# The first two steps of a scan-and-feed-forward kernel on half of the tokens, with the other half's scan between them

## The chip, the cores and the metric

The kernel runs on one core of one Trainium2 chip. Its time is the device time of one execution in microseconds (us). Before the change three executions took 386.27, 387.29 and 387.14 us; the median is 387.14 us. The execution that the profiler recorded has a span of 384.9 us, and all times inside it count from the start of that span.

## The reference

Two blocks follow each other. The first is a Mamba-2 style scan (SSD) over x of 4 sequences, 8 heads, 768 positions, head width 32, with a state of width 16; the second is a feed-forward block with a gate, over the 3072 rows that come out.

```
for each chunk:                       # the reference uses chunks of 32, the kernel of 128
    cum = cumsum(log(clip(a)))
    M   = (C @ B.T) * exp(cum_i - cum_j) * (i >= j)
    y   = M @ x  +  (C @ state) * exp(cum_i)
    state = exp(sum) * state + sum_j B_j x_j exp(cum_last - cum_j)

x2 = y as 3072 rows of 256            # 4 sequences x 768 positions, 8 heads x 32
h  = x2 @ w_in                        # 256 -> 2048
g  = h * cos(h)
out = g @ w_out                       # 2048 -> 256
```

The weights w_in and w_out arrive as 64-bit floats, everything else as 32-bit ones.

## The kernel before, in words

**Tiling.** A chunk is 128 positions of all four sequences, so 512 tokens; there are NC = 6 chunks. Inside a chunk the feed-forward block runs in NF = 16 steps. A step n takes one half u of the tokens (two sequences, 256 tokens) and one pair j of the 16 column blocks of w_in (256 of the 2048 hidden columns). `first(n)` makes h for them: four matmuls of 128x256, two (over the halves of the 256 inputs) for each block e of the pair. Then ScalarE makes k, the whole turns in h (`L516`), VectorE the rest of the turn, w (`L518`), ScalarE the cosine (`gate`, `L523`) and VectorE the product gT (`gated`, `L528`). `second(n)` multiplies gT with w_out into an accumulator in PSUM; it stands two steps behind its `first` (LAG = 2).

**The order is written by hand.** The kernel is built under a manual schedule: each engine runs its instructions in the order in which the Python code calls them. [...]

**The start.** Chunk 0 has no state behind it, and its scan is done sequence by sequence (b = 0 to 3) ahead of the first step. For one sequence: `spread_a` (TensorE puts a's decays in place), `decays0` (one VectorE scan, `L308`, then two GpSimd instructions, `L311` and `L312`), `turn` (TensorE turns B and C, ScalarE makes cT twice and bT of them), `cross` (one matmul for two sequences, and two ScalarE copies into lam, `L320`), `intra` (four matmuls g, then two VectorE products m, `L380`), and `finish` (eight matmuls y, and a ScalarE copy into yT, `L394`, which is the operand of `first`). `weigh` (GpSimd, `L327`) prepares `sum_up`, the matmuls that make the chunk's state; `carry` stores that state for the next chunk. `fill` is a matmul without use that keeps TensorE busy.

**The weights.** Each weight comes in eight pieces of 512 KB (`fetch`). A piece is turned into 32-bit floats by `grade` (ScalarE `L193` and `L191`, GpSimd `L194`) and `join` (VectorE `L207` and `L209`, GpSimd `L217`). The first piece of w_in is graded in two shares. Piece i of w_in holds the columns of the pair j = i; piece i of w_out the rows of the pair j = i.

**Before the change** all four scans stand ahead of `first(0)`, except `finish(3)` and the states, which stand right behind it. In chunk 0 the steps take the halves in turn: `turn_of` gives n = 0 the pair 0 of the first half, n = 1 the pair 0 of the second half, n = 2 the pair 1 of the first half, and so on. So the second piece of w_in is first used at n = 2, and the second half of the tokens at n = 1. All loads go through one queue in the order of the code: B, C and x of the sequences 0, 1 and 2, the first piece of w_in, B, C and x of sequence 3, a_in, and then pieces of both weights in turn. `a_in` is all of a; from it GpSimd makes `cut` and `la`, which go back to memory as a_cut and a_all and are read again as the decays of the chunks from 1 on.

**Buffers.** PSUM is held by tags with two buffers each: "h" for the results of `first` (and at the start for spread_a and turn), "o" for those of `second` (and at the start for cross and finish), and "scan", two buffers of two banks, for g, tp and the states.

Of the kernel before, what the change touches and what calls it, by code (L numbers as in the profile page):

```python
# [25 lines left out]
def kernel(  # L26
# [29 lines left out]
    nc = tc.nc  # L56
    V, ACT, G, PE = nc.vector, nc.scalar, nc.gpsimd, nc.tensor

    NB, H, S, D = x.shape
# [48 lines left out]
    def load(c, seqs=(0, NB)):  # L108

        if c >= NC:  # L110
            return
        if c not in raw:
            raw[c] = (loads.tile([P, 2, NB * H, N], FP32, tag="bc", name="bc"),
                      loads.tile([P, NB, H, D], FP32, tag="xr", name="xr"))
        bc, xr = raw[c]
        xr = xr.rearrange("p b h d -> p (b h) d")
        rs = slice(seqs[0] * H, seqs[1] * H)
        for dst, src in ((bc[:, 0, rs], B), (bc[:, 1, rs], C), (xr[:, rs], x)):
            nc.sync.dma_start(out=dst, in_=src[seqs[0]:seqs[1], :, c * P:(c + 1) * P, :]
                              .rearrange("b h s n -> s (b h) n"))  # L120
# [96 lines left out]
            G.tensor_tensor(out=dst.bitcast(U32), in0=bits, in1=last, op=ALU.add)  # L217

    for b in range(NB):
        if b == NB - 1:  # L220
            fetch("in", 0)
        load(0, (b, b + 1))
    nc.sync.dma_start(
        out=a_in, in_=a.rearrange("(u b) h (c p) -> (b h c) u p", u=NU, p=P))
    for w in (("in", 1), ("out", 0), ("in", 2), ("out", 1), ("in", 3)):
        fetch(*w)


# [73 lines left out]
    def decays0(b):  # L302
# [8 lines left out]
        G.tensor_copy(out=l[W:P, 1], in_=l[W:P, 0])  # L311
        G.memset(l[W:P, 0], 0.0)  # L312

    def cross(b, tag):

        ps = bank([P, H, W], "l_ps", tag)
        PE.matmul(ps, lhsT=fros[:, b:b + 2].rearrange("p b j -> p (b j)"), rhs=tos,
                  start=True, stop=True)
        for t in range(2):
            ACT.copy(out=lam[0, b + t][0:W, 1], in_=ps[t * W:(t + 1) * W])  # L320
            weigh(0, b + t)

    def weigh(c, b):

        scaled[c, b] = sc = scan.tile([P, H, N], FP32, tag="sc", bufs=NB, name="sc")
        l = lam[c, b][:, :, P - 1:P] if c > 0 else lam[c, b][:, 1, :, W - 1:W]
        G.tensor_tensor(out=sc, in0=raw[c][0][:, 0, heads(b)],  # L327
                        in1=l.to_broadcast([P, H, N]), op=ALU.mult)
# [21 lines left out]
            return  # L350
        weigh(c, b)

    def turn(b, tag=None):

        bc = raw[0][0]
        tp = (pair("tp")[:, 0] if tag is None else bank([P, 4 * P], "tp", tag)
              ).rearrange("p (k i) -> p k i", k=4)
        for k in range(2):
            PE.transpose(tp[:, k], bc[:, k, heads(b)].rearrange("p h n -> p (h n)"), ident)

        cT = scan.tile([P, 2, P], FP32, tag="cT", name="cT")
        for t in range(2):
            ACT.activation(cT[:, t], tp[:, 1], AF.Copy, scale=slot[:, t:t + 1])
        bT = scan.tile([P, P], FP32, tag="bT", name="bT")
        ACT.copy(out=bT, in_=tp[:, 0])
        part[0, b] = (bT, cT)

    def intra(b):
        bT, cT = part[0, b]
        g = [pair("g") for _ in range(2)]  # L370
        for q in range(4):
            r = slice(32 * q, 32 * q + 32)
            PE.matmul(g[q // 2][:, q % 2, 0:2 * P], lhsT=bT[r],
                      rhs=cT[r].rearrange("p t (s i) -> p s t i", s=2), start=True, stop=True)
        l = lam.pop((0, b))
        m = scan.tile([P, 2, H, W], FP32, tag="m", name="m")
        for q in range(2):
            of = [t[:, :, q * HH:(q + 1) * HH].rearrange("p s (k t) i -> p k s (t i)", k=2)
                  for t in (m, l)]
            V.tensor_tensor(out=of[0], in0=g[q][:, :, 0:2 * P].rearrange(  # L380
                "p k (s i) -> p k s i", s=2), in1=of[1], op=ALU.mult)
        part[0, b] = m

    def finish(b, tag, fills=0):
        m, xr = part.pop((0, b)), raw[0][1]
# [111 lines left out]
    def turn_of(n):  # L497

        c, f = divmod(n, NF)
        return (f % 2, f // 2) if c == 0 else divmod(f, NJ)  # L500

    def first(n):
# [6 lines left out]
        for e in range(2):  # L509
            fs = slice((2 * j + e) * P, (2 * j + e + 1) * P)  # L510
            for k in range(KT):
                PE.matmul(to_[:, e], lhsT=w_in[:, k, fs], rhs=y[:, k, u],  # L512
                          start=(k == 0), stop=(k == KT - 1), skip_group_check=True)
# [142 lines left out]

    warm = bank([P, 4, P], "warm", "o")
    fill(warm, 2)
    fill(warm[:, 0:2])
    spread_a(0, "h")  # L660
    turn(0)
    spread_a(1, "h")
    spread_a(2, "o")
    spread_a(3, "h")
    for b in range(NB):
        decays0(b)
    turn(1, "h")
    cross(0, "o")
    intra(0)
    turn(2, "h")  # L670
    cross(2, "o")
    intra(1)
    finish(0, "o")
    grade("in", 0, n=2)
    intra(2)
    turn(3, "h")
    finish(1, "o", 1)

    la = const.tile([RB, NU, P], FP32, name="la")
    cut = const.tile([RB, NU, P], FP32, name="cut")  # L680
# [7 lines left out]
    join("in", 0)  # L688
    finish(2, "o")
    intra(3)  # L690
    grade("in", 1)
    join("in", 1)


    piece = {n: ("in", (n + 3) // 2) if n % 2 else ("out", n // 2) for n in range(NF)}
# [12 lines left out]

    def first_scan():

        finish(3, "o")
# [21 lines left out]
    def halves_at(n):  # L733
        return [(c, b, t) for c in range(1, NC) for u in range(2)
                for m, b, t in ahead.get(c, {}).get(u, halves_of[u]) if m + (c - 1) * NF == n]

    EARLY = 3
    rest_of_loads()
    for n in range(NC * NF + LAG):
        c, f = divmod(n, NF)  # L740
        early = n < EARLY
        if n < NC * NF:
            if f == 0 and c > 0:
                load(c + 2)
            first(n)
            if n == 0:
                first_scan()
            for at in pairs(n):
                turn2(*at)
            rests = [grade(*piece[m], later=True)  # L750
                     for m in ((n,) if early else ()) + ((n + 1,) if n >= EARLY - 1 else ())
                     if m in piece]
            gate(n)
            for rest in rests:
                if rest:
                    rest()
            if not early and n in piece:
                join(*piece[n])
            gated(n)
            if early and n in piece:  # L760
                join(*piece[n])
            if n in (1, 2):
                carry(0, n - 1, sums[n - 1])
        for i, js in differ_at.get(n, ()):
            differ_w(i, js)
        if n >= LAG:
            second(n - LAG)
        for c, u in pairs(n - 1):
            intra2(c, u)
            masked(c, 2 * u)  # L770
        for c, u in pairs(n - 2):
            masked(c, 2 * u + 1)
        for c, u in pairs(n - 3):
# [41 lines left out]
```

## Time and profile before

| what | value |
|---|---|
| time, median of 3 | 387.14 us (386.27 to 387.29) |
| span of the profiled execution | 384.9 us |
| TensorE busy (matmul) | 378.3 us, 98% |
| VectorE busy | 265.9 us, 69% |
| GpSimd busy | 245.4 us, 64% |
| ScalarE busy | 172.9 us, 45% |
| first matmul of `first(0)` | at 18.80 us |
| first matmul of `second(0)` | at 26.55 us |

The busy time of TensorE is a share of the whole span. The change touches only the first 30 us or so, and there the question is what TensorE does in each stretch, and what it waits for. So the rows to read are those of the start, in order of time, and the list of what TensorE waited for after the start.

### The profile page before, as it was taken

The page shows a single profiled execution, that of the slowest core. Times are in us where ns is not written, and L with a number is a line of the kernel's source. Part 1 is how long each engine was busy: PE and PEld are TensorE (multiplying, and loading weights), DVE is VectorE, ACT ScalarE, POOL GpSimd, SP SyncE. Part 2 cuts the span into 40 slices and gives each one's busy share as a digit, 9 for nine tenths or more (in the row PEclk, how much of TensorE's full clock was granted, in tenths as well). Part 3 has the DMA queues.
Part 4 walks back from the last instruction along what each step waited for, and adds up shares of the span by engine and source line. Part 5 has one row for each costly group of instructions (what it writes and reads, how often), then busy time and mean ns, then how long its engine had stood idle before and what let it go on. Part 6 is the DMA issues. An engine that isn't in the chain of part 4 may idle for free.

```text
span 384.9 us, 7726 instructions
## 1 busy us (share of the span) xinstructions
PE 378.3 (98%) x2982; PEld 331.2 (86%) x2982; DVE 265.9 (69%) x395; ACT 172.9 (45%) x303; POOL 245.4 (64%) x366
## 2 busy tenths in 40 slices
PE   8999999999999999999999999999999999999996
PEld 3578887888899899899899899899899989989995
DVE  7879999678667658657657757756765865863443
ACT  3878566534334334335334434434433433433441
POOL 5757665458859549648648837855955855853751
PEclk9999999999999999999999999999999999999999
DMA  7989899975002951301791301201210000010001
GB/s 83 270 235 266 249 230 137 181 96 151 2 0 63 148 52 57 96 2 54 127 81 55 97 2 56 81 17 43 68 43 1 21 10 0 2 27 3 7 22 27
DMA packets 106371, 30.42 MB, mean 79 GB/s; under 512 B 75520, under 2 KB 102240, under 8 KB 106336
## 3 DMA queue, kind: packets, MB, share of 16 engines
q1 hardware_dynamic: 106176, 29.81, 38.9%
q8 instruction: 23, 0.38, 0.5%
q10 hardware_dynamic: 160, 0.13, 0.1%
q14 instruction: 12, 0.10, 0.1%
HBM read 26.59 MB, written 3.34 MB: 78 GB/s over the span
## 4 chain that ended last, share of the span: by engine, by line
PE 82%; DVE 7%; POOL 3%; ACT 2%; issue 2%; DMA 2%; SPq 1%; ACTq 0%
PE hp L512 37%; PE o L609 32%; PE g L422 3%; PE y L454 3%; DVE mag L209 2%; DVE w L518 2%; DMA xr<-in_x_dram 2%; PE y L447 2%; DVE lam L344 2%; PE o L571 1%; DVE gT L528 1%; PE warm L101 1%; ACT w L523 1%; PE a_ps L298 1%; PE tp L405 1%
## 5 line engine op out<-in xcount | busy, mean ns | idle before, releaser
L512 PE MATMUL hp<-yT,w_in 128*128 128x256 f32 x768 | 184.4, 383 | 0.6 <-POOL w_in L217 0.3
L512 PEld LDWEIGHTS hp<-yT,w_in 128*128 128x128 f32 x768 | 139.2, 190 | 22.7 <-issue 4.5
L553 POOL TENSOR_TENSOR gd<-gT 128x256 f32<-128x256 f32 x79 | 71.9, 911 | 89.5 <-DVE gT L528 86.2
L528 DVE TENSOR_TENSOR gT<-hp,w 128x512 f32<-128x512 f32 x96 | 66.3, 691 | 69.9 <-ACT w L523 60.1
L523 ACT ACTIVATE w<-w,quarter 128x512 f32<-128x512 f32 x96 | 69.3, 722 | 97.2 <-DVE w L518 97.2
L516 ACT ACTIVATE k<-hp 128x512 int32<-128x512 f32 x96 | 57.1, 595 | 90.8 <-PE hp L512 90.7
L518 DVE SCALAR_TENSOR_TENSOR w<-hp,k 128x512 f32<-128x512 f32 x96 | 65.4, 681 | 36.7 <-ACT k L516 36.4
L609 PE MATMUL o<-words,gd 128*128 128x128 f32 x474 | 67.0, 277 | 0.6 <-POOL gd L555 0.6
L609 PEld LDWEIGHTS o<-words,gd 128*128 128x128 f32 x474 | 59.3, 192 | 2.4 <-POOL gd L555 2.2
L344 DVE TENSOR_TENSOR_SCAN lam<-arow,unit 128x512 f32<-128x512 f32 x40 | 55.7, 1394 | 0.0
L609 PEld LDWEIGHTS o<-w_out,gT 128*128 128x128 f32 x316 | 46.9, 191 | 3.6
L609 PE MATMUL o<-w_out,gT 128*128 128x128 f32 x316 | 48.0, 274 | 0.0
L555 POOL TENSOR_TENSOR gd<-gT,gd 128x128 f32<-128x128 f32 x79 | 43.1, 546 | 6.2
L556 POOL TENSOR_TENSOR gd<-gT,gd 128x128 f32<-128x128 f32 x79 | 35.9, 455 | 6.2
L571 PE MATMUL o<-w_out,gT 128*128 128x256 f32 x128 | 30.3, 380 | 0.4 <-POOL w_out L217 0.4
L609 PE MATMUL o<-w_out,gd 128*128 128x128 f32 x158 | 30.6, 275 | 0.0
L609 PE MATMUL o<-words,gT 128*128 128x128 f32 x158 | 30.5, 275 | 0.0
L571 PEld LDWEIGHTS o<-w_out,gT 128*128 128x128 f32 x128 | 24.2, 190 | 4.0 <-POOL w_out L217 0.8
L435 DVE TENSOR_TENSOR m<-g,lam 128x512 f32<-128x512 f32 x40 | 25.6, 681 | 0.0
L624 POOL TENSOR_TENSOR sum<-ps,sum 128x256 f32<-128x256 f32 (+1 forms) x27 | 24.2, 909 | 1.4
L609 PEld LDWEIGHTS o<-w_out,gd 128*128 128x128 f32 x158 | 24.0, 192 | 0.0
L609 PEld LDWEIGHTS o<-words,gT 128*128 128x128 f32 x158 | 24.0, 192 | 0.0
(91 smaller groups left out, 293.9 us busy)
## 6 DMA issues: line engine op xcount, KB each, us to landing
arow<-a_cut SPq DMA_DIRECT2D x20, 512.0 KB
words<-in_moe_w_in_dram SPq DMA_DIRECT2D x8, 512.0 KB
words<-in_moe_w_out_dram SPq DMA_DIRECT2D x8, 512.0 KB
out_dram<-sum SPq DMA_DIRECT2D x18, 128.0 KB
xr<-in_x_dram SPq DMA_DIRECT2D x4, 512.0 KB
along<-a_all SPq DMA_DIRECT2D x20, 64.0 KB
xr<-in_x_dram SPq DMA_DIRECT2D x8, 128.0 KB
bc<-in_B_dram SPq DMA_DIRECT2D x4, 256.0 KB
```

The costliest lines, as they stand in the source:

```text
L344: V.tensor_tensor_scan(out=lam[c, b][:, hs].rearrange("p h i -> p (h i)"), data0=rows_.rearrange("p h i -> p (h i)"), data1=unit.rearrange ...
L435: V.tensor_tensor(out=of[0], in0=g[q][:, :, s * 2 * P:(s + 1) * 2 * P], in1=of[1], op=ALU.mult)
L512: PE.matmul(to_[:, e], lhsT=w_in[:, k, fs], rhs=y[:, k, u], start=(k == 0), stop=(k == KT - 1), skip_group_check=True)
L516: ACT.activation(k, hp[n], AF.Copy, bias=0.25, scale=INV_2PI)
L518: V.scalar_tensor_tensor(out=w, in0=hp[n], scalar=INV_2PI, in1=k, op0=ALU.mult, op1=ALU.subtract)
L523: ACT.activation(cos, cos, AF.Sin, bias=quarter, scale=TWO_PI)
L528: V.tensor_tensor(out=gT[n], in0=hp.pop(n), in1=cos, op=ALU.mult)
L553: G.tensor_tensor(out=d[:, 0:2], in0=g[:, 1:2].to_broadcast([P, 2, P]), in1=g[:, 3::-3], op=ALU.subtract)
L555: G.tensor_tensor(out=d[:, 2], in0=g[:, 0], in1=d[:, 0], op=ALU.subtract)
L556: G.tensor_tensor(out=d[:, 3], in0=g[:, 2], in1=d[:, 2], op=ALU.subtract)
L571: PE.matmul(o[c, u][:, t], lhsT=g[:, 2 * e + t], rhs=w_out[:, 2 * j + e], start=(j == e == t == 0), stop=(j == NJ - 1 and e == 1), skip_gr ...
L609: PE.matmul(at[q], lhsT=a_[q], rhs=w[q], start=(j == 0 and q in starts), stop=(j == NJ - 1), skip_group_check=True)
```

## The change

The kernel goes on to compute the same. Four things are moved.

- **The steps.** `turn_of` gives the first four steps of chunk 0 as (half 0, pair 0), (half 0, pair 1), (half 1, pair 0), (half 1, pair 1). So the first two steps need the sequences 0 and 1 alone, and they need two pieces of w_in.
- **The scan.** Only sequences 0 and 1 are scanned ahead of `first(0)`. `decays0` of sequences 2 and 3 stays ahead of it, and the rest of their scan is put between the parts of the first two steps by a new function `start`: `turn(2)` and `cross(2)` between the two halves of `first(0)`, `intra(2)` behind it, `turn(3)` between the two halves of `first(1)`, then `intra(3)`, `finish(2)`, `finish(3)` and the states. `turn(3)` writes into the unused half of a bank that holds g of sequence 2. `cross` is split: the matmul stays in it, the two copies go to `crossed`; the four `weigh` stand behind `gated(0)`.
- **The loads.** Two pieces of w_in are fetched behind sequence 1, ahead of sequences 2 and 3; a_in goes behind sequence 2, and then come two pieces of w_out and two of w_in.
- **The weights at the start.** Both first pieces of w_in are graded and joined ahead of `first(0)`. The first piece of w_out is graded behind `gated(0)` and joined at the end of `start`; the other pieces of the first steps are graded one step later than before. The fills change: one ahead of the scan goes, and `finish(0)` and `finish(1)` get one and two (before: none and one). `carry` of chunk 0 goes from n = 1 and 2 to n = 4 and 5.

The purpose is to let `first(0)` begin before the second pair of sequences has been loaded and scanned.

```
     for b in range(NB):
-        if b == NB - 1:
+        load(0, (b, b + 1))
+        if b == 1:
             fetch("in", 0)
-        load(0, (b, b + 1))
-    nc.sync.dma_start(
-        out=a_in, in_=a.rearrange("(u b) h (c p) -> (b h c) u p", u=NU, p=P))
-    for w in (("in", 1), ("out", 0), ("in", 2), ("out", 1), ("in", 3)):
+            fetch("in", 1)
+        if b == 2:
+            nc.sync.dma_start(
+                out=a_in, in_=a.rearrange("(u b) h (c p) -> (b h c) u p", u=NU, p=P))
+    for w in (("out", 0), ("out", 1), ("in", 2), ("in", 3)):
         fetch(*w)
...
-        return (f % 2, f // 2) if c == 0 else divmod(f, NJ)
+        if c > 0:
+            return divmod(f, NJ)
+        return divmod(f, 2) if f < 4 else (f % 2, f // 2)
...
     warm = bank([P, 4, P], "warm", "o")
     fill(warm, 2)
-    fill(warm[:, 0:2])
     spread_a(0, "h")
-    turn(0)
     spread_a(1, "h")
+    turn(0, pair("tp")[:, 0, 0:2 * P])
+    decays0(0)
+    decays0(1)
+    cross(0, "o")
+    crossed(0)
+    crossed(1)
     spread_a(2, "o")
+    intra(0)
+    turn(1, bank([P, 2 * P], "tp", "h"))
+    decays0(2)
     spread_a(3, "h")
...
+    finish(0, "o", 1)
+    grade("in", 0, n=2)
     intra(1)
...
+    grade("in", 1)
+    finish(1, "o", 2)
+    join("in", 0)
+    join("in", 1)
+    decays0(3)
...
+    def start():
+
+
+        def then():
+            turn(2, pair("tp")[:, 0, 0:2 * P])
+            cross(2, "o")
+            crossed(2)
+        first(0, then)
+        crossed(3)
+        g = intra(2)
+        first(1, lambda: turn(3, g[0][:, 0, 2 * P:4 * P]))
+        gate(0)
+        gated(0)
+        for b in range(NB):
+            weigh(0, b)
+        rest = grade("out", 0, later=True)
+        intra(3)
+        for b in range(NB):
+            del lam[0, b]
+        finish(2, "o")
+        gate(1)
+        finish(3, "o")
+        first_scan()
+        gated(1)
+        for w in (("out", 1), ("in", 2)):
+            held_back.append(grade(*w, later=True))
+        if rest:
+            rest()
+        join("out", 0)
...
-            if n in (1, 2):
-                carry(0, n - 1, sums[n - 1])
+            if n in (4, 5):
+                carry(0, n - 4, sums[n - 4])
```

More of the change, by code (lines that the diff above doesn't have):

```diff
@@ L312, in decays0, with crossed @@
         G.memset(l[W:P, 0], 0.0)
+    crosses = {}
     def cross(b, tag):
-        ps = bank([P, H, W], "l_ps", tag)
+        crosses[b] = ps = bank([P, H, W], "l_ps", tag)
         PE.matmul(ps, lhsT=fros[:, b:b + 2].rearrange("p b j -> p (b j)"), rhs=tos,
                   start=True, stop=True)
-        for t in range(2):
-            ACT.copy(out=lam[0, b + t][0:W, 1], in_=ps[t * W:(t + 1) * W])
-            weigh(0, b + t)
+    def crossed(b):
+        t = b % 2
+        ACT.copy(out=lam[0, b][0:W, 1], in_=crosses[b - t][t * W:(t + 1) * W])
     def weigh(c, b):
@@ L351, in decays, with turn @@
         weigh(c, b)
-    def turn(b, tag=None):
+    def turn(b, tp):
         bc = raw[0][0]
-        tp = (pair("tp")[:, 0] if tag is None else bank([P, 4 * P], "tp", tag)
-              ).rearrange("p (k i) -> p k i", k=4)
+        tp = tp.rearrange("p (k i) -> p k i", k=2)
         for k in range(2):
@@ L374, in intra @@
                       rhs=cT[r].rearrange("p t (s i) -> p s t i", s=2), start=True, stop=True)
-        l = lam.pop((0, b))
+        l = lam[0, b]
         m = scan.tile([P, 2, H, W], FP32, tag="m", name="m")
@@ L382, in intra @@
         part[0, b] = m
+        return g
     def finish(b, tag, fills=0):
@@ L499, in turn_of, with first @@
         c, f = divmod(n, NF)
-        return (f % 2, f // 2) if c == 0 else divmod(f, NJ)
-    def first(n):
+        if c > 0:
+            return divmod(f, NJ)
+        return divmod(f, 2) if f < 4 else (f % 2, f // 2)
+    def first(n, between=None):
         c, f = divmod(n, NF)
@@ L509, in first @@
         for e in range(2):
+            if e and between:
+                between()
             fs = slice((2 * j + e) * P, (2 * j + e + 1) * P)
@@ L658 @@
     fill(warm, 2)
-    fill(warm[:, 0:2])
     spread_a(0, "h")
-    turn(0)
     spread_a(1, "h")
+    turn(0, pair("tp")[:, 0, 0:2 * P])
[4 more added lines that the diff above has]
+    crossed(1)
     spread_a(2, "o")
+    intra(0)
+    turn(1, bank([P, 2 * P], "tp", "h"))
+    decays0(2)
     spread_a(3, "h")
[L665 to L671, printed above, removed]
-    intra(1)
[L673 to L677, printed above, removed]
+    finish(0, "o", 1)
+    grade("in", 0, n=2)
+    intra(1)
+    grade("in", 1)
[3 more added lines that the diff above has]
+    decays0(3)
     la = const.tile([RB, NU, P], FP32, name="la")
@@ L686 @@
             out=dst.rearrange("(u b) h (c p) -> (b h c) u p", u=NU, p=P), in_=src)
[L688 to L692, printed above, removed]
     piece = {n: ("in", (n + 3) // 2) if n % 2 else ("out", n // 2) for n in range(NF)}
@@ L709, in first_scan @@
     def first_scan():
-        finish(3, "o")
         for u in range(2):
@@ L735, in halves_at @@
                 for m, b, t in ahead.get(c, {}).get(u, halves_of[u]) if m + (c - 1) * NF == n]
+    def start():
[25 more added lines that the diff above has]
+        join("out", 0)
+    held_back = []
     EARLY = 3
     rest_of_loads()
+    start()
     for n in range(NC * NF + LAG):
@@ L744 @@
                 load(c + 2)
+            if n < 2:
+                continue
             first(n)
-            if n == 0:
-                first_scan()
             for at in pairs(n):
                 turn2(*at)
-            rests = [grade(*piece[m], later=True)
-                     for m in ((n,) if early else ()) + ((n + 1,) if n >= EARLY - 1 else ())
-                     if m in piece]
+            rests = [grade(*piece[n + 1], later=True)] if n + 1 in piece else []
+            if early:
+                rests = held_back + rests
             gate(n)
@@ L756 @@
                     rest()
-            if not early and n in piece:
+            if n in piece:
                 join(*piece[n])
             gated(n)
-            if early and n in piece:
-                join(*piece[n])
-            if n in (1, 2):
-                carry(0, n - 1, sums[n - 1])
+            if early:
+                join("in", 2)
+            if n in (4, 5):
+                carry(0, n - 4, sums[n - 4])
         for i, js in differ_at.get(n, ()):
```

## The prediction

> **What bounds the kernel now.** I read the page first, for the share of each engine.
>
> ```profile
> PE 378.3 (98%) x2982; PEld 331.2 (86%) x2982; DVE 265.9 (69%) x395; ACT 172.9 (45%) x303; POOL 245.4 (64%) x366
> ```
>
> TensorE (PE) has work for 98% of the span. Next, what TensorE waited for from 30 us to the end (columns: total us, times, longest us).
>
> ```profile
> PE o L609 <- POOL gd L555: 0.6, 1, 0.6
> PE hp L512 <- DVE gT L528: 0.2, 1, 0.2
> ```
>
> 0.8 us in 355 us: after the start the kernel is one unbroken line of matmuls. Whatever moves the first `second` moves the end by the same amount, if the matmuls behind it stay the same. That makes the start the only place to look: TensorE's rows from 12 us on (start, length, name, idle before).
>
> ```profile
> 18.80 2.29 PE L512 MATMUL hp<-yT,w_in 128*128 128x256 f32 x8 [0.32 <-POOL w_in L217]
> 21.02 0.65 PE L390 MATMUL y<-m,xr 128*32 128x128 f32 x16
> 21.48 0.63 PE L471 MATMUL s_ps<-xr,sc 128*32 128x64 f32 x32
> 22.15 3.98 PE L512 MATMUL hp<-yT,w_in 128*128 128x256 f32 x16
> 26.55 1.99 PE L571 MATMUL o<-w_out,gT 128*128 128x256 f32 x8 [0.42 <-POOL w_out L217]
> 28.38 1.89 PE L512 MATMUL hp<-yT,w_in 128*128 128x256 f32 x8
> ```
>
> `first(0)` begins at 18.80, `first(1)` and `first(2)` fill 22.15 to 26.1, `second(0)` begins at 26.55. At that moment both kernels have done the same matmuls: the scan of chunk 0, three `first`, no `second`. From there the line is the same in both, so I compare one number: the start of `second(0)`. Last, the rows of the other engines that I use as prices, and that show who was late.
>
> ```profile
> 16.93 0.29 DVE L207 TENSOR_SCALAR mag<-mag 128x256 uint32<-128x256 uint32 x1
> 17.34 0.60 POOL L683 TENSOR_SCALAR la<-a_in 96x256 f32<-96x256 f32 x1
> 18.02 0.73 POOL L217 TENSOR_TENSOR w_in<-mag,last 128x256 uint32<-128x256 uint32 x1
> 18.12 0.91 DVE L209 SCALAR_TENSOR_TENSOR mag<-words,mag 128x256 uint32<-128x256 uint32 x1
> 22.57 0.72 ACT L523 ACTIVATE w<-w,quarter 128x512 f32<-128x512 f32 x1
> 23.33 0.69 DVE L528 TENSOR_TENSOR gT<-hp,w 128x512 f32<-128x512 f32 x1 [0.88 <-ACT w L523]
> 25.23 1.27 POOL L217 TENSOR_TENSOR w_out<-mag,last 128x512 uint32<-128x512 uint32 x1 [1.43 <-DVE mag L209]
> ```
>
> The first share of w_in is written by GpSimd from 18.02 to 18.75, and `first(0)` follows at 18.80: it waits for a weight, whose conversion stood behind the scan on VectorE and behind `la` on GpSimd. `second(0)` waits for its weight too (25.23 + 1.27 = 26.50).
>
> [...] the first share's `L194` was done at 15.95, but its `L207` began at 16.93, behind two products m on VectorE. My chain below rests on this. [...] `L209` took 0.43 us for the first share and 0.91 for the second, beside `L217`. [...]
>
> **Part 1: an earlier `first(0)`.** I walk the new order with the durations of the trace: an instruction starts when its engine is free and its last releaser is done, plus 0.02 to 0.08 us. Prices: one 128x256 matmul 0.43 us (a `first` and a `second` together repeat every 3.45 us, eight matmuls), spread_a 0.86, turn 0.38 on TensorE and 0.93 on ScalarE (cT, cT, bT), cross 0.86, intra 0.68, finish 0.62, fill 0.47, states 0.63, lam 1.2, m 2x0.645. The same walk through the old order puts `first(0)` at 18.4 and `second(0)` at 26.0; the trace has 18.80 and 26.55, so the walk is right to about half a us.
>
> TensorE: spreads 0 and 1, turn(0), cross(0), spread(2), intra(0) end at 9.5. VectorE: m(0) 9.4 to 10.7, lam of sequence 2 to 11.9. TensorE: turn(1), spread(3), a fill, finish(0), intra(1) to 12.5. VectorE: m(1) 12.2 to 13.5; finish(1) ends at 14.05. The two w_in pieces landed at 12.1 and 17.3 before; behind sequence 1, whose x landed at 8.4, I estimate 10.0 and 11.4 (1.4 to 1.65 us each there), so they don't bind. What binds is the conversion: ScalarE turns to it after the copy of y(0), at 12.3; GpSimd is held by lam of sequence 2 to 13.2; VectorE joins the first share to 14.6; GpSimd grades the second piece first (to 15.05) and writes the share 15.1 to 15.8. `first(0)` at 15.9, [...] **16.2, 2.6 us earlier** than 18.80.
>
> **Part 2: the scan that moved behind it.** TensorE now has between `first(0)` and `second(0)`, beyond the old 6.45 us (three `first` 5.2, finish 0.62, states 0.63): two turns 0.76, cross 0.86, two intra 1.36, finish(2) 0.62. That is **3.6 us more**, all on TensorE's line. By itself this and part 1 give +1.0 us.
>
> **Part 3: what TensorE waits for there.** One chain runs through three engines[...]:
> - `first(0)` 16.2, its first half to 17.1, turn(2) and cross(2) to 18.3, its second half to 19.2;
> - k(0) on ScalarE to 19.85; w(0) on VectorE, which stands ahead of m(2), to 20.55; first m(2) to 21.25;
> - turn(3): its bank belongs to g of sequence 2, and in the built program it waits for that first m(2). On TensorE the second half of `first(1)` stands behind it. TensorE is idle about 0.6 us; turn(3) ends at 21.7, `first(1)` at 22.55;
> - ScalarE: cT, cT, bT to 22.7, and only then k(1) to 23.35 and the cosine of step 0, which was ready to go since 20.6, to 24.1;
> - VectorE: gT(0) waits for that cosine, to 24.85, and m(3) stands behind gT(0): 26.2;
> - finish(3) needs m(3): 26.5; TensorE did intra(3) and finish(2) before 24.0 and idles about 1.8 us;
> - yT and the states, in parallel: **`first(2)` at 27.2**; before it was 24.1.
>
> `first(2)` ends at 28.9. `second(0)` needs the first piece of w_out: on VectorE its join stands behind gT(1) (27.2 to 28.4); on ScalarE its `last` stands behind two other pieces' `mag`: 27.0 + 3x0.68 = 29.05; GpSimd grades those two pieces first and then writes it, 1.27: 30.4. **`second(0)` at 30.5**, TensorE idle another 1.6 us.
>
> **The sum.** 30.5 - 26.55 = 3.95. By parts: start -2.6, work moved +3.6, idle 4.25 in place of 1.3, +2.95. I forecast 387.14 + 4.0 = **391.1 us**.
>
> **Costed at nothing.** The fill removed at the start: the scan waits for a0s until 4.3 anyway (ScalarE's four `L277` end there). The two fills added run while VectorE makes m. `carry` later: two 0.28 us products, next read in chunk 1. a_cut is sent at about 20 instead of 17.3, behind `decays0(3)` on GpSimd, and the queue of loads behind it; but old loads were still landing until 22.7, and readers shift by 4 us too.
>
> **Rivals.**
> - *Waits close up* (faster). If the piece were ready when y(1) is, `first(0)` starts at 14.5; with all idle time gone, 14.5 + 10.05 = 24.55: 385.1 us. For it: matmuls exist to fill the gaps. Against: the order puts w(0), gT(0) and turn(3) in series. 6%.
> - *Absorbed*. VectorE is busy for 9.6 to 9.9 us of each 10 from 30 to 60 us; were it the real pace there, a late TensorE would catch up: about +1, 388.1 us. Against: TensorE's steps stand 3.45 us apart there without a wait. 9%.
> - *The w_out piece comes in time* and only `first(2)` counts: +3.1 - 0.4 (the old wait there) = +2.7, 389.8 us. 15%.
> - *Worse*: [...] another 2 us, 393.1 us. 12%.
> - My forecast: 58%.
>
> **Range and chances.** 388.8 to 393.0 holds the forecast, the late-weight case and about half of the worse one; below lie the first two cases. Faster by over 0.3% (under 385.98): 6%. Within 0.3%: 8%. Slower: 86%.
>
> **What would show each step.** Right: `first(0)` near 16.2; turn(3) behind an idle TensorE released by m; a wait of 1 to 2 us of y on m; `second(0)` near 30.5 released by GpSimd's w_out; no TensorE waits after. Wrong: `second(0)` before 27, or new waits after 31.

## The result, and the profile after

The changed kernel took 390.74 us (median of four executions, 390.00 to 391.81); the kernel before, run beside it, 387.07 us. The ratio is 1.0101, with a 95% interval of 1.0073 to 1.0128: it is slower. A second run of the same kernel on another occasion gave 389.73 against 386.59 us, 1.0094 (1.0076 to 1.0111). The forecast was 391.1 us.

The page of the changed kernel, first line of shares and the line of the granted TensorE clock:

```profile
PE 380.0 (97%) x2984; PEld 331.8 (85%) x2984; DVE 266.8 (68%) x395; ACT 172.8 (44%) x303; POOL 244.8 (63%) x366
PEclk9989999999999999999999999999999999999999
```

The work is the same but for two more matmul records of fills. TensorE's busy time rose by 1.7 us and the span by 4.9 us, and the third digit of the clock is an 8. This profiled execution was the slowest of the four (391.81 us) and the only one with a mean clock below 1.00 (0.994). In the profile of the second run TensorE is busy for 377.7 us, so the rise is not work; it goes with the lower clock. I read the order of the waits from this second run: its profiled execution (389.49 us) had a granted clock of 1.00 in all of the first 60 us. The clock comes back below. TensorE's rows of the second run (start, length, name, idle before and its releaser; the trace has two records for each matmul of the code, so one `first` is x8):

```profile
15.98 1.13 PE L521 MATMUL hp<-yT,w_in 128*128 128x256 f32 x4 [1.43 <-POOL w_in L217]
...
18.98 0.71 PE L377 MATMUL g<-cT,bT 32*128 32x256 f32 x8
...
21.06 0.44 PE L363 MATMUL g<-ident,bc 128*128 128x128 f32 x2 [0.30 <-DVE m L384]
...
24.99 0.43 PE L395 MATMUL y<-m,xr 128*32 128x128 f32 x8 [1.27 <-DVE m L384]
25.58 0.42 PE L395 MATMUL y<-m,xr 128*32 128x128 f32 x8 [0.17 <-DVE m L384]
...
26.50 1.99 PE L521 MATMUL hp<-yT,w_in 128*128 128x256 f32 x8
29.59 1.99 PE L580 MATMUL o<-w_out,gT 128*128 128x256 f32 x8 [1.09 <-POOL w_out L217]
...
35.06 1.99 PE L521 MATMUL hp<-yT,w_in 128*128 128x256 f32 x8
```

`first(0)` begins at 15.98 where it began at 18.80, and `second(0)` at 29.59 where it began at 26.55. So 2.8 us are won at the start, and from there to `second(0)` it takes 13.61 us in place of 7.75, 5.9 us more. New in this stretch are the scan of the second pair (the row at 18.98 is intra(2)) and three waits: 0.30 for turn(3), 1.27 and 0.17 for y on m, 1.09 for the first piece of w_out. The 2.8 us hold for these two executions only, since the first microseconds of the changed kernel scatter by more than 1 us from execution to execution (last section); the 13.61 us lie behind that scatter.

The same stretch on ScalarE shows why y waits:

```profile
21.59 0.63 ACT L367 ACTIVATE cT<-g,slot 128x128 f32<-128x128 f32 x2 [1.29 <-PE g L363]
...
22.40 0.60 ACT L525 ACTIVATE k<-hp 128x512 int32<-128x512 f32 x1
22.90 0.71 ACT L532 ACTIVATE w<-w,quarter 128x512 f32<-128x512 f32 x1
```

And on VectorE:

```profile
23.64 0.69 DVE L537 TENSOR_TENSOR gT<-hp,w 128x512 f32<-128x512 f32 x1
24.25 1.28 DVE L384 TENSOR_TENSOR m<-g,lam 128x512 f32<-128x512 f32 x2
```

The cosine of step 0 stands behind cT, bT and k(1) on ScalarE and ends at 23.61; gT(0) follows at 23.64, m(3) at 24.25, the first y at 24.99. Each row starts about when the one above it ends.

The first profile differs from the end of the scan on. TensorE had half clock there (0.50 from 26.49 to 29.90 us), and its rows are:

```profile
27.83 3.00 PE L521 MATMUL hp<-yT,w_in 128*128 128x256 f32 x8
30.67 1.95 PE L580 MATMUL o<-w_out,gT 128*128 128x256 f32 x8
```

`first(2)` took 3.00 us in place of 1.99, and `second(0)` followed with no listed wait for w_out. This profile did have waits after 31 us (columns: total us, times, longest us):

```profile
PE o L580 <- POOL w_out L217: 0.7, 1, 0.7
PE o L618 <- POOL gd L564: 0.6, 1, 0.6
PE hp L521 <- POOL w_in L217: 0.4, 1, 0.4
```

The second line was there before the change. The other two are the second piece of w_out and the third piece of w_in, in the steps 3 and 4.

### The profile page after: what moved, and what is told of

Read it like the earlier page. It is cut to its first block, busy times and chain, and to the rows that moved or that the text cites. A ratio compares the mean times of both kernels' runs of the same rounds, so it can differ in the third digit from the quotient of the medians.

```text
span 389.8 us, 7733 instructions
## 1 busy us (share of the span) xinstructions
PE 380.0 (97%) x2984; PEld 331.8 (85%) x2984; DVE 266.8 (68%) x395; ACT 172.8 (44%) x303; POOL 244.8 (63%) x366
## 4 chain that ended last, share of the span: by engine, by line
PE 90%; DVE 4%; POOL 3%; ACT 2%; issue 1%; ACTq 0%; POOLq 0%
PE hp L521 41%; PE o L618 31%; PE o L580 5%; PE g L427 3%; PE y L459 3%; PE y L452 2%; PE a_ps L300 1%; PE tp L410 1%; PE warm L101 1%; POOL words L556 1%; DVE w L527 1%; DVE lam L349 1%; PE s_ps L476 1%; ACT k L525 1%; POOL gd L562 1%
## 5 line engine op out<-in xcount | busy, mean ns | idle before, releaser
L618 PE MATMUL o<-w_out,gd 128*128 128x128 f32 x158 | 30.5, 275 | 0.0
```

What stands on the lines that cost most here:

```text
L618: PE.matmul(at[q], lhsT=a_[q], rhs=w[q], start=(j == 0 and q in starts), stop=(j == NJ - 1), skip_group_check=True)
```

## The experiments

**My theory:** the time goes in two parts: the second pair's matmuls now lie between `first(0)` and `second(0)`, and TensorE waits there, for the chain of turn(3), gT(0) and m(3) (the *links*) and for pieces of the weights that are wanted before their conversion is through the queues. **Rivals:** the half clock of the first profile; the new order of the loads; the second pair's matmuls alone.

To set the runs side by side I use one more row than the forecast did, `first(4)` (the first matmul of step 4): the order of the feed-forward steps is again that of the kernel before from there on. In the kernel before it is this row:

```profile
31.83 1.89 PE L512 MATMUL hp<-yT,w_in 128*128 128x256 f32 x8
```

Start times are from the profiles and medians from the timed executions, in us. The column "fill to first(4)" counts from the first fill of `finish(0)`, which lies behind the part of the start that scatters; the kernels with the old start have no entry. The last column is the median less that of the kernel before beside it.

| kernel | first(0) | second(0) | first(4) | fill to first(4) | span | median less before |
|---|---|---|---|---|---|---|
| before | 18.80 | 26.55 | 31.83 | | 384.9 | |
| changed, first run | 16.81 | 30.67 | 37.44 | 25.95 | 389.8 | +3.67 |
| changed, second run | 15.98 | 29.59 | 35.06 | 24.40 | 387.6 | +3.14 |
| turn(3) in a bank of its own | 16.25 | 29.57 | 36.34 | 25.41 | 388.8 | +3.27 |
| m(3) ahead of gT(0) | 16.15 | 29.68 | 35.17 | 24.34 | 387.6 | +2.94 |
| w_out's first piece first | 16.39 | 29.07 | 35.51 | 24.44 | 387.9 | +3.12 |
| these three together | 16.05 | 28.18 | 34.48 | 23.75 | 386.9 | +2.42 |
| three together, and w_in's first piece earlier | 15.90 | 28.17 | 34.47 | 23.17 | 386.5 | +1.79 |
| the last, three pieces not converted | 16.47 | 27.83 | 33.01 | 21.13 | 384.9 | -0.19 |
| changed, three pieces not converted | 17.45 | 29.80 | 34.98 | 22.85 | 386.9 | +1.83 |
| changed, second pair not scanned | 16.10 | 27.79 | 33.94 | 23.15 | 386.7 | +2.18 |
| changed, gaps filled | 17.29 | 30.88 | 36.37 | 24.41 | 388.8 | +3.64 |
| before, step order alone | 19.23 | 27.25 | 37.94 | | 390.3 | +5.86 |
| before, load order alone | 19.11 | 26.86 | 32.15 | | 385.3 | +0.89 |

In every kernel with the new step order the span less `first(4)` is 351.9 to 352.8 us, and 353.1 in the kernel before. So what is lost is lost ahead of `first(4)`, and nothing is lost behind it. Half clock came between the fill and `first(4)` in three of these profiles (first run, own bank, second pair not scanned; the figures are in the last section).

**1. turn(3) in a bank of its own.**

```
-        first(1, lambda: turn(3, g[0][:, 0, 2 * P:4 * P]))
+        first(1, lambda: turn(3, bank([P, 2 * P], "tp", "o")))
```

> Changed kernel with turn(3) in a bank of its own, so that it no longer waits for the first product m(2). Theory [...]: TensorE's 0.3 to 0.6 us wait ahead of turn(3) goes, and all behind it, second(0) too, comes about 0.65 us earlier: ratio to the kernel before about 1.0085 (changed kernel 1.010). Rival (the waits are slack; VectorE's joins in the steps 2 to 4 set the pace): no difference, 1.010.

389.95 us, 1.0092 (1.0069 to 1.0115). The wait of turn(3) on m is gone from the list, as expected, but y on m stays at 1.4, the profiled execution also lost clock (mean 0.994), like the first run, and `second(0)` (29.57) is not the 0.65 us earlier that I expected. Ahead of the half clock the link does show:

```profile
24.73 0.43 PE L395 MATMUL y<-m,xr 128*32 128x128 f32 x8 [1.26 <-DVE m L384]
```

From `first(0)` to this row it took 8.48 us, in the second run 9.01. By its time alone the experiment decides nothing: its interval holds the ratio of the changed kernel.

**2. m(3) ahead of gT(0).** The rest of step 0 is moved behind `intra(3)`.

```
         first(1, lambda: turn(3, g[0][:, 0, 2 * P:4 * P]))
-        gate(0)
-        gated(0)
...
-        rest = grade("out", 0, later=True)
         intra(3)
+        gate(0)
+        gated(0)
+        rest = grade("out", 0, later=True)
```

> Changed kernel with gate(0) and gated(0) behind intra(3), so that on VectorE the products m(3) stand ahead of gT(0). Theory: y of sequence 3 waits for m(3) 0.7 us less, second(0) comes about 0.7 us earlier: ratio about 1.008. Rival: no difference, 1.010, since gT(0) and the first piece of w_out come 0.7 us later and second(0) waits for them instead.

389.62 us, 1.0080 (1.0066 to 1.0093). The waits of its TensorE from 5 to 60 us:

```profile
PE o L580 <- POOL w_out L217: 1.6, 1, 1.6
...
PE y L395 <- DVE m L384: 0.8, 2, 0.7
```

y on m fell from 1.4 to 0.8 us and the wait for w_out grew from 1.1 to 1.6: what one wait gives, the next takes. `second(0)` did not move (29.68). The ratio is the one that the theory gave, but its interval overlaps that of the changed kernel, and the profile shows what the rival said.

**3. The first piece of w_out ahead of the two others.**

```
-        for w in (("out", 1), ("in", 2)):
-            held_back.append(grade(*w, later=True))
         if rest:
             rest()
         join("out", 0)
+        for w in (("out", 1), ("in", 2)):
+            held_back.append(grade(*w, later=True))
```

> Changed kernel in which the first piece of w_out is finished (its last part on ScalarE, then its join) ahead of the grading of the two next pieces. Theory: GpSimd writes it about 1 us earlier, the wait ahead of second(0) falls from 1.6 us to about 0.6, but second(1) then waits about 0.4 us for the second piece: 0.6 us net, ratio about 1.0085. Rival: the two pieces held back come that much later and take all of it back: 1.010.

389.80 us, 1.0088 (1.0073 to 1.0103). TensorE's rows:

```profile
29.07 1.99 PE L580 MATMUL o<-w_out,gT 128*128 128x256 f32 x8 [0.17 <-POOL w_out L217]
...
33.09 1.99 PE L580 MATMUL o<-w_out,gT 128*128 128x256 f32 x8 [0.30 <-POOL w_out L217]
35.51 1.99 PE L521 MATMUL hp<-yT,w_in 128*128 128x256 f32 x8 [0.42 <-POOL w_in L217]
```

The wait ahead of `second(0)` is 0.17 in place of 1.09, and the two pieces that were put behind now come late, for `second(1)` and for `first(4)`. Again the end does not move: from the fill to `first(4)` it took 24.44 us, in the second run 24.40. By the profile the rival was right; the ratios of the two, 1.0085 and 1.010, the timing can't tell apart.

**4. The three together.**

> The three edits of the other runs together. Theory: the links are in one chain, so they add up to about 1.7 us: 389.0 us, ratio about 1.005; TensorE's waits between first(0) and second(0) fall from about 4 us to about 2.5. Rival (slack): 1.010. Rival (the idle time is the whole of the loss): below 1.003.

389.10 us, 1.0071 (1.0056 to 1.0087). It was to give 1.005. TensorE's rows:

```profile
28.18 1.99 PE L580 MATMUL o<-w_out,gT 128*128 128x256 f32 x8 [0.75 <-POOL w_out L217]
...
34.48 1.99 PE L521 MATMUL hp<-yT,w_in 128*128 128x256 f32 x8 [0.43 <-POOL w_in L217]
```

`second(0)` is 1.4 us earlier than in the second run, `first(4)` only 0.6 (counted from the fill, 0.65): the third piece of w_in is now what ends last. The gain in time, 0.7 us, is of the size of that row, though the intervals of the two kernels overlap.

**5. The step order alone, in the kernel before.**

```
-        return (f % 2, f // 2) if c == 0 else divmod(f, NJ)
+        if c > 0:
+            return divmod(f, NJ)
+        return divmod(f, 2) if f < 4 else (f % 2, f // 2)
```

> Kernel before with the new order of the first four steps alone; scan, loads and conversions stay. Its first(0) stays at 18.8. Theory: the new order needs the second piece of w_in one step earlier and the second piece of w_out one step earlier, and these are converted in the old order, so TensorE waits about 1 us ahead of first(1) and about 4 us ahead of second(1), less what it saved elsewhere: about 3.7 us, ratio 1.0095. Rival (the step order is free, the loss is the scan between the steps): 1.000 to 1.002.

392.10 us, 1.0157 (1.0140 to 1.0174): slower, as expected, and by more than half as much again. TensorE's rows:

```profile
23.70 3.72 PE L514 MATMUL hp<-yT,w_in 128*128 128x256 f32 x16 [1.16 <-POOL w_in L217]
...
34.64 3.46 PE L573 MATMUL o<-w_out,gT 128*128 128x256 f32 x8 [3.77 <-POOL w_out L217]
```

With pair 1 in step 1, the second piece of w_in is wanted one step earlier (it makes TensorE wait 1.16 us) and the second piece of w_out too (3.77 us). ScalarE's list of waits from 18 to 42 us has no transfer in it, so the pieces are late by their conversion. Behind that gap the next eight records took 3.46 in place of 1.89 us: half clock (a mean of 0.55 from 34.64 to 38.00 us). It costs 1.57 us of the 5.86, the expectation had left it out, and all four timed executions had a mean clock of 0.991 to 0.994. Of the parts that I ran alone this is the dearest: it asks for weights sooner than the kernel converts them.

**6. The load order alone, in the kernel before.** Only the loads are moved as in the changed kernel.

> Kernel before with the new order of the loads alone. Theory: B and C of sequences 2 and 3 land about 3 us later than before, which holds turn(2) up by about 1 us ahead of the first step; the conversion of w_in is bound by VectorE and GpSimd as before; first(0) about 0.5 us later, ratio about 1.0015. Rival (late loads are a main part of the loss): 1.004 or more.

387.13 us, 1.0020 (1.0012 to 1.0028). `first(0)` and `second(0)` are both 0.3 us later. In the kernel before, the load order is no cause of this size; in the changed kernel it was not tried alone. If 5 and 6 simply added up they would give +6.8 us, where the whole change gives 3.1 to 3.7. Of this difference of 3.1 to 3.6 us, 1.6 are the half clock of experiment 5; the other 1.5 to 2 us would be what the earlier start and the earlier conversion of the weights win back. That they add up is not shown.

**7. The changed kernel with three pieces not converted.** ScalarE fills the first two pieces of w_out and the third of w_in with a constant ahead of the scan; all else stays.

```
+        if (which, i) in (("out", 0), ("out", 1), ("in", 2)):
+            return
```

> Changed kernel without the conversion of the first two pieces of w_out and the third of w_in: ScalarE fills these pieces with a constant before the scan, so the output is not the reference's. Theory: the wait of 1.6 us ahead of second(0) and the ones of the steps 1 to 4 go; what is left is the scan's chain: first(2) at about 27.5, second(0) right behind it at about 29.1; ratio about 1.0055. Rival (the conversions are the whole loss): 1.000 or below. Rival (they are slack): 1.010.

388.07 us, 1.0052 (1.0034 to 1.0070), near the theory's 1.0055 and clear of the second run's 1.0076 to 1.0111. Three of its ten timed executions had a mean clock of 0.996 and took 389.38 to 389.72 us; the other seven have a median of 387.58 us, 1.3 us above the kernel before. The whole list of TensorE's waits from 5 to 60 us is now:

```profile
PE y L407 <- DVE m L396: 1.4, 2, 1.3
PE hp L533 <- POOL w_in L222: 1.4, 1, 1.4
PE g L375 <- DVE m L396: 0.3, 1, 0.3
```

The wait for w_out is gone: from `first(0)` to `second(0)` it took 12.35 us in place of 13.61. `first(0)` is later (17.45), but not through the constants. ScalarE had written them by 6.17 us and then waited for the first turn:

```profile
8.35 0.62 ACT L379 ACTIVATE cT<-tp,slot 128x128 f32<-128x128 f32 x2 [2.18 <-PE tp L375]
```

From the first fill of `finish(0)` to `first(0)` it took 5.32 us, as in the second run; the delay lies ahead of it, in the scatter of the start (last section). In the second run ScalarE's list of waits from 18 to 45 us has no transfer in it, so these pieces had landed when ScalarE came to them; what is late is their conversion.

**8. The three together, and the first piece of w_in earlier.** Its two shares are graded ahead of `decays0(2)`, the first share is joined ahead of m(1) (`join` takes the number of the share as a third argument), and the second piece is graded after the first is joined.

```
     turn(1, bank([P, 2 * P], "tp", "h"))
+    grade("in", 0, n=2)
     decays0(2)
     spread_a(3, "h")
+    join("in", 0, 0)
     finish(0, "o", 1)
-    grade("in", 0, n=2)
     intra(1)
-    grade("in", 1)
     finish(1, "o", 2)
-    join("in", 0)
+    join("in", 0, 1)
+    grade("in", 1)
     join("in", 1)
```

> The three edits of e4, and the first share of w_in converted ahead of finish(0) and m(1) rather than behind them. Theory: first(0) waits for y of sequence 1 rather than for the weight and starts near 15.5 rather than 16.1 to 16.8; the chain behind it moves with it: second(0) about 1 us earlier than in e4, ratio about 1.004; still slower than before, since the 3.6 us of scan on TensorE are there. Rival (the start of first(0) doesn't matter, a later link such as the loads of sequence 3 or the weights does): 1.007 as e4.

388.03 us, 1.0050 (1.0036 to 1.0065). This is the best version that leaves nothing out, clearly better than the change and still slower than the kernel before. `first(0)` no longer waits for the weight but for yT:

```profile
15.90 1.10 PE L523 MATMUL hp<-yT,w_in 128*128 128x256 f32 x4 [0.58 <-ACT yT L401]
```

From the first fill of `finish(0)`, at 11.30, it is 4.60 us to `first(0)`; in the second run of the changed kernel it was 5.32 (from 10.66). So the start is 0.7 us earlier, though the table's start time hides it, since executions differ in their first microseconds (last section). Against experiment 4 the intervals overlap, and `second(0)` begins at the same time; counted from the fill, `first(4)` is 0.6 us earlier (23.17 for 23.75), where about 1 us was expected.

**9. The changed kernel again.**

> The changed kernel once more, beside the next three on one chip. All theories: ratio about 1.010; this narrows its interval. In the earlier profile TensorE ran at about two thirds of its clock from 26 to 31 us; if that belongs to the kernel, this profile shows it too.

1.0094 (1.0076 to 1.0111), told above. The profile has a clock of 1.00 from 26 to 31 us, so the half clock of the first one does not belong to every execution.

**10. Gaps filled.** Three fills behind `finish(1)` and three ahead of `finish(3)`, so that TensorE doesn't idle.

```
     finish(1, "o", 2)
+    spare = pair("spare")[:, 0, 0:2 * P].rearrange("p (k i) -> p k i", k=2)
+    fill(spare, 3)
...
-        finish(3, "o")
+        finish(3, "o", 3)
```

> Changed kernel with three more fills behind finish(1) and three ahead of finish(3), where TensorE is idle for 1.4 and 1.3 us. Theory (the waits set the time; the half clock is a rare extra of single executions): same as the changed kernel, 1.010, with a smaller spread of its executions. Rival [...]: 1.007 or less, and no slice under full clock.

390.23 us, 1.0104 (1.0085 to 1.0122). The mean clock of its four timed executions was 0.999 to 1.000, and it is no faster: the 1.007 of the rival lies below the interval. Nor are they closer together, as I had expected: they took 389.67 to 390.92 us. From `first(0)` to `second(0)` it took 13.59 us (13.61 without the fills), with the wait for w_out at 1.08, and from the fill to `first(4)` 24.41 us (24.40). So the half clock is not where the time goes; neither is it needed for the loss, as the second run had a clock of 1.00 there and nearly the same ratio (1.0094).

**11. The second pair not scanned.** The output of the first pair is copied in its place, and the decays of the first pair are used for the states.

```
-        first(0, then)
-        crossed(3)
-        g = intra(2)
-        first(1, lambda: turn(3, g[0][:, 0, 2 * P:4 * P]))
+        first(0)
+        first(1)
+        lam[0, 2], lam[0, 3] = lam[0, 0], lam[0, 1]
...
-        finish(3, "o")
+        ACT.copy(out=yT[0][:, :, 2 * P:4 * P], in_=yT[0][:, :, 0:2 * P])
```

> Changed kernel that leaves out turn, cross, intra and finish of sequences 2 and 3; their y is a copy of that of 0 and 1, and their states take the decays of 0 and 1, so the output is not the reference's. Theory: 3.6 us of TensorE and the scan's waits go, but the first piece of w_out and what is queued on GpSimd and ScalarE then set second(0): it starts at about 27, no earlier than before the change; ratio 1.001. Rival (the moved scan is the whole loss, the earlier start is a real gain): second(0) at about 24, ratio 0.993.

388.77 us, 1.0070 (1.0054 to 1.0085). I had expected about 1.001. Turn, cross, intra and finish of two sequences are gone, and still the kernel is slower than before. TensorE's rows:

```profile
19.26 1.99 PE L521 MATMUL hp<-yT,w_in 128*128 128x256 f32 x8 [0.83 <-POOL w_in L217]
22.13 1.44 PE L476 MATMUL s_ps<-xr,sc 128*32 128x64 f32 x32 [0.88 <-POOL sc L332]
24.23 3.10 PE L521 MATMUL hp<-yT,w_in 128*128 128x256 f32 x8 [0.66 <-ACT yT L755]
27.79 2.27 PE L580 MATMUL o<-w_out,gT 128*128 128x256 f32 x8 [0.46 <-POOL w_out L217]
...
33.94 1.99 PE L521 MATMUL hp<-yT,w_in 128*128 128x256 f32 x8 [0.43 <-POOL w_in L217]
```

Where the scan was there are waits for weights, for GpSimd's sc and for the copy, which neither kernel has. `first(4)` came only 1.1 us earlier than in the second run. With experiment 7, which takes away the conversions and leaves the scan, this fits two paths of nearly the same length: taking one away leaves the other. This execution also had half clock, from 25.0 to 28.4 us (the rows of 3.10 and 2.27 us; last section), but that does not seem to hold the kernel: of its five timed executions the one with a clock of 1.00 took 388.58 us, 0.2 us below the median.

**12. Experiment 8 with three pieces not converted.** The edits of 7 and 8 together.

> The kernel e8 (three links cut, first share of w_in ahead) without the conversion of the first two pieces of w_out and the third of w_in, which are filled with a constant; the output is not the reference's. Theory: TensorE goes from first(0) at about 16 to second(0) at about 27.2 with 1.2 us of idle time, and no wait after: ratio about 1.0015. So even with the weights for nothing the change would only draw level: 3.6 us of scan moved against 2.6 to 3 us of earlier start. Rival (the weights are the whole rest of the loss): 0.997 or less.

386.40 us, 0.9999 (0.9990 to 1.0008). Its TensorE rows:

```profile
16.47 1.10 PE L535 MATMUL hp<-yT,w_in 128*128 128x256 f32 x4 [0.58 <-ACT yT L413]
...
27.83 1.89 PE L594 MATMUL o<-w_out,gT 128*128 128x256 f32 x8
```

With most waits cleared and part of the work left out, the change draws level with the kernel before, slightly better than the 1.0015 of the theory; the rival's 0.997 lies outside the interval. `second(0)` is 1.3 us later than before. The kernel before was not run without these conversions. It waits 0.42 us for one of these pieces, so the comparison is not quite like with like.

## Why the prediction was right

The forecast, 391.1 us, lies 0.4 us from the median of the first run and 1.4 us from that of the second; as a difference it was +4.0 us, and the two runs gave +3.7 and +3.1. The direction and the chain of causes up to `second(0)` were as said. That the first profile comes so near is in part luck: `second(0)` began at 30.67 there, where 30.5 was forecast, but without the wait for w_out that was to put it there. The half clock, for which the forecast's sum has no term, took its place. Point by point:

- **An earlier `first(0)`**: forecast 16.2, measured 16.81 and 15.98. It is released as forecast: in the second run GpSimd grades the second piece and then writes the first share, from 15.17 to 15.93 us. The walk had 15.1 to 15.8 for this. The walk itself ends with `first(0)` at 15.9; the 0.3 us that the forecast has on top of that were its author's estimate, and whether they were needed can't be told, since the start scatters by more than that.
- **The scan that moved**: forecast 3.6 us of TensorE's line. From `first(0)` to `first(4)` the kernel before took 13.03 us, of which 0.42 are a wait; experiment 12 took 16.54 with 0.83 of listed waits. That is 3.1 us more work; experiment 7 gives 3.2 in the same way, the second run of the changed kernel 3.6, with gaps too small to be listed. So the term is right or up to 0.5 too high. The forecast's count of the old stretch was low, though: it took 6.45 us as work and 1.3 us as idle time, but only 0.42 us are listed as a wait, which leaves 7.33 us of matmuls and small gaps. By the same count the second run has 10.78 us up to `second(0)`, where the forecast had 10.05. Experiment 11 adds what the sum didn't say: these 3.6 us are not on the path alone; take them away and weights take most of their place.
- **The waits**: three were forecast, in this order, with these releasers, and all three are there in the second run, each smaller: turn(3) 0.30 (forecast 0.6), y on m 1.44 with its second part (1.8), w_out 1.09 (1.6). Together 2.83 us for 4.0. `second(0)` came at 29.59 in the second run and not at 30.5, for three reasons: waits 1.4 us below the 4.25 us of idle time in the sum, matmuls and small gaps 0.7 us above it, and a start 0.2 us earlier. The errors cancel in part. The chain ran through the rows named: "cT, cT, bT", then k(1), the cosine, gT(0), m(3). In the second run they began in the order of the code: k(1) at 22.40, the cosine at 22.90, gT(0) at 23.64, m(3) at 24.25. Experiment 2 agrees: putting m(3) ahead of gT(0) took 0.6 us off that wait.
- **"no TensorE waits after"**: this failed. In the first run, and in experiments 1, 3, 4, 8 and 11, the third piece of w_in makes `first(4)` wait 0.42 to 0.43 us, and in the first run and experiments 1 and 3 the second piece of w_out makes `second(1)` wait 0.3 to 0.7 us. The second run has no such wait in its list, but only just. VectorE's join of the third piece of w_in:

```profile
31.95 1.64 DVE L209 SCALAR_TENSOR_TENSOR mag<-words,mag 128x512 uint32<-128x512 uint32 x1
```

And GpSimd's write of that piece:

```profile
33.74 1.27 POOL L217 TENSOR_TENSOR w_in<-mag,last 128x512 uint32<-128x512 uint32 x1 [0.69 <-DVE mag L209]
```

GpSimd is done at 35.01 and `first(4)` begins at 35.06. The join on VectorE took 1.64 us, where the same instruction took 0.69 at 30.22. Beside it, from 31.56 to 33.05, GpSimd was writing a piece of w_out; whether that made the join longer isn't shown, since no run takes this write alone away. The walk stopped at `second(0)`; the conversion queue did not.
- **No time for a lower clock**: the forecast's sum has none, and this failed too, in part. In three profiles of the changed kernel and its variants the clock was halved for a stretch (0.50 from 26.49 to 29.90 us in the first run). Where it came it cost some 1.5 us: from the fill to `first(4)` the first run took 25.95 us, the second 24.40. Experiment 10 shows that it doesn't make the loss.
- **One row decides the end**: `second(0)` was 3.04 us later in the second run and the span 2.7 us longer; in experiment 12 it was 1.3 us later and the span the same. So the line behind is not quite rigid: some 0.3 to 1.3 us are made up. I can point to part of it: TensorE of the kernel before is idle 0.80 us between 60 and 120 us, that of experiment 12 only 0.55, and the wait of 0.2 us for gT is gone. The rest I did not find.

**How the loss divides**, from medians less those of the kernel before beside them: +3.1 us for the change (second run); putting the links and the first w_out piece in better order makes it +2.4, the earlier first piece of w_in +1.8; leaving out three conversions makes it -0.2. So about 1.3 us are order and 2.0 us are the conversion of three pieces. The intervals of neighbours overlap in the first two of these three steps. The profiles, counted from the fill to `first(4)`, give the same split without the scatter of the start: 1.2 us for the order and 2.0 for the conversions. Experiment 7, which leaves the conversions out in the plain change, gives 1.3 us for them by its median, which three executions at a lower clock push up, and 1.55 us by the fill. So the two shares overlap by some tenths, and the split is no finer than that. What remains is the bare exchange, in experiment 12 a start 2.3 us earlier against 3.5 us more from there to `first(4)`; the line behind makes up the difference. Two points stay open: the part of the make-up not found, and what the kernel before would gain from leaving out the same conversions.

## What to carry to other kernels

A step that can start earlier is worth only what its followers can use. Before moving one, count the work that thereby slides between it and the next step, and look, for each of the next four or five operands, where its preparation stands in the program's order on each engine that works on it. When several such chains end within a us of each other, shortening one only names the next, so price the whole set; and one reordered index (here the pair of each step) may be the dearest line of the change, because it sets when each operand is due.

## What the runs showed of the hardware that I had not expected

**Half clock behind waits of at most 1.28 us.** The first run, in stretches (length, busy us and count of TensorE, of its weight load, of VectorE, ScalarE and GpSimd, then granted clock, DMA share, GB/s):

```profile
22.50:24.50 2.00, 1.95 (x28) 0.96 (x26) 0.64 (x2) 1.96 (x6) 1.40 (x4) 1.00 0.39 98
24.50:26.49 1.99, 0.54 (x16) 0.23 (x16) 1.99 (x5) 1.37 (x3) 0.61 (x1) 1.00 0.91 270
26.49:28.20 1.71, 1.71 (x41) 1.54 (x42) 1.49 (x3) 1.10 (x3) 0.05 (x1) 0.50 1.08 120
28.20:29.90 1.70, 1.70 (x5) 1.33 (x5) 0.00 (x0) 0.99 (x2) 1.70 (x3) 0.50 0.81 196
```

From 26.49 to 29.90, 3.41 us, TensorE had half clock. In the 4 us ahead of it, it was busy for 2.5 us and its longest wait was 1.28 us. So here 1.5 us of idle time in 4 us, in pieces of at most 1.28 us, were followed by half clock. It isn't sure to follow: the second run had waits of nearly the same lengths up to there (0.30, 1.27 and 0.17 us) and a clock of 1.00. What makes the difference isn't shown. The slow stretch was about as long in the other profiles that have one. I estimate its ends from the mean clock of their windows, taking it as 0.50 inside the stretch: 25.4 to 28.8 us in experiment 1 (0.92 from 22 to 26 us, 0.72 from 26 to 31), 25.0 to 28.4 in experiment 11 (0.87 and 0.76 in the same windows), and 34.2 to 37.7 in experiment 5 (0.95 from 30.87 to 34.64, 0.55 from 34.64 to 38.00), there at the end of a wait of 3.77 us.

**The start differs between executions.** The first eight records of spread_a, in the first run and then in the second:

```profile
4.77 2.53 PE L300 MATMUL a_ps<-a0s,those 128*64 128x512 f32 x8
4.53 1.94 PE L300 MATMUL a_ps<-a0s,those 128*64 128x512 f32 x8
```

The first fill of `finish(0)` began at 11.49 and 10.66. From that fill to `first(0)` both took 5.32 us. So the 0.8 us between the two starts of `first(0)` arose in TensorE's first 7 us, ahead of the waits that are discussed here; the recorded clock is 1.00 in both, so its cause isn't shown. Over the eleven profiles of the changed kernel and its variants these eight records took 1.94 us (three profiles and the second run) to 3.16 us (experiment 7), and the fill began between 10.66 and 12.13. A start time in the table is no finer than that.
